# Three inverse jobs moved from the end of an FFT convolution into its last tiles, and two reloads moved ahead of outputs

## The chip, the cores and the metric

One core of a Trainium2 chip runs the kernel; the other seven are idle. The metric is the device time of one execution in microseconds (us), the median of several runs. The core has five engines that run side by side, each in its own program order: TensorE (PE, with its weight loads shown as PEld), VectorE (DVE), ScalarE (ACT), GpSimd (POOL) and SyncE (SP). SP does nothing here but issue DMA transfers.

## The reference

A 7x7 circular convolution over a 224x224 image with 96 input and 96 output channels, written as a product of two-dimensional Fourier transforms:

```python
H = W = 224; C = 96; K = 7
def reference(x, w):                       # x (1,224,224,96), w (7,7,96,96), bf16
    wp = jnp.pad(w, ((0, H - K), (0, W - K), (0, 0), (0, 0)))
    Xf = rfft2(x.astype(float32), axes=(1, 2))
    Wf = rfft2(wp.astype(float32), axes=(0, 1))
    Yf = jnp.einsum('bhwi,hwio->bhwo', Xf, Wf)
    return irfft2(Yf, s=(H, W), axes=(1, 2)).astype(bfloat16)
```

The output is 224 x 224 x 96 in bf16, 9.6 MB.

## The kernel before

**Tiling.** The image rows are cut into 8 blocks of 28 (`NJ`, `B`). Each block is transformed along the rows with a short Fourier transform of length 34 (`L`), which gives 17 frequencies (`NS`). Along the columns the kernel works directly with the seven taps, two output columns at a time. The columns are cut into 7 tiles of 32 pixels; the code counts them t = 0 to 6, and this text does too, so "the fifth tile" is tile 4, "the sixth" tile 5, and "the last" tile 6 (`TL`).

**Three stages for each tile.**

1. The forward transform (`a_jobs`): products of pixels with the constant matrix `Fm` on PE, copied from PSUM to `xf`. It runs one tile ahead, so nothing of it is left to do during tile 6.
2. 17 rounds (`b_round`), one for each frequency s. A round is 33 products of PE, 19 into a first PSUM bank and 14 into a second one, with operands that are pieces of `xf` or of sums `J` that DVE makes for three frequencies at a time (`jit`, two buffers). ACT scales the first bank into `tt_`, DVE makes `u` and `v` from the banks, and POOL or DVE adds them up to `yf`. After two or three rounds `yf` is written to a scratch tensor in HBM (`scr`, in the last tile seven smaller ones, `scrl`).
3. The inverse transform (`c_jobs`): the scratch is read back as `tt` with another order of axes (`load_t`), multiplied on PE by the constant matrix `Gm`, copied from PSUM to an output buffer (`yo`, or two halves of the third `J` buffer), and written to the output. There are 11 jobs for each tile, 0 to 10. They use five reloads: jobs 0 and 1 use (0,0), 2 and 3 use (1,0), 4 to 6 use (2,0), 7 and 8 use (0,1), 9 and 10 use (1,1). A job is two products of 384 columns and two copies of 384 elements per partition. The jobs 1, 3, 8 and 10 write 252 KB of output each, job 5 writes 252 KB in three transfers and job 6 writes 84 KB.

**How the jobs are placed.** Every round has two places where filling work is put: `mid`, between the two banks, and `end`. With k = 2s and 2s + 1 a tile has 34 such places. `pace` spreads a list of jobs evenly from place a to place b. For each tile, `CQ[t] = (nold, nnew)` says how many jobs left over from tile t - 2 and how many of tile t - 1 are done while the rounds of tile t run. The rest of tile t - 1 is left over for tile t + 1. The old jobs stand from place 3 to a place `km`, the new ones from `km` to the end; in tile 6 `km` is 13 and the end is 26. What is left over in tile 6 stands behind its rounds (`cj` after `tail[0] = 2`); there each product is followed by a second one of the same size with zeros (`wu`), which adds nothing, and the copies go to DVE and ACT in turn.

**The end.** The inverse of tile 6 is done differently: its scratch is reloaded in seven parts (`load_p(0)` to `load_p(6)`, into a free `xf` buffer), each as soon as its rounds are written. `load_p(5)` belongs to rounds 14 and 15, whose write POOL issues, and `load_p(6)` to round 16, whose write ACT issues. `first` multiplies the parts 0 to 2 (matrix `GA`); eight such products are made as soon as there are banks. Then come `WARM` = 12 products with zeros, and then `second` multiplies the parts 3 to 6 (matrix `GB`) and adds them in the same banks, DVE and ACT copy, and SP writes the output in eight transfers.

**Queues.** All reloads, all outputs and the scratch writes of the tiles 0 to 5 are issued by SP in one order; an instruction that waits holds up all behind it. Every DMA of SP has one of eight semaphores in turn, so it also waits for the one that stood eight places ahead of it.

Of the kernel before, what the change touches and what calls it, by code (L numbers as in the profile page):

```python
# [36 lines left out]
YBUF = 4  # L37
JGB = ((0, 3), (3, 6), (6, 9), (9, 12), (12, 15), (15, 17))
LAG = 4
CQ = {2: (11, 0), 3: (11, 2), 4: (9, 5), 5: (6, 8), 6: (3, 4)}  # L40
SH2 = {0: (0, 8, 17), 1: (0, 8, 17), 2: (0, 8, 13, 17)}
MERGE = ()
NP2 = 0
# [9 lines left out]
def kernel(  # L53
# [84 lines left out]
    def dma(out_ap, in_ap):  # L138
        return DE.dma_start(out=out_ap, in_=in_ap)
# [278 lines left out]
    def a_jobs(t):  # L418
        xf = new_xf(t)
        jobs = []  # L420
        for jg in range(2):
            for h in range(2):
                for (q, n) in ((0, 3), (3, 3), (6, 2)):
                    jobs.extend(a_bank(t, xf, xn_bufs[jg], h * PXC + 2 * q, n, jg, HALO + h * 8 + q))
            jobs.append(then_load(jobs.pop(), t + 1, jg))
        return jobs
# [182 lines left out]
    def load_p(i):  # L609
        a, b, h, r0 = prt[i]  # L610
        sv = scr_tiles[(TL, i)].rearrange("w j s (r e) -> (j s r) w e", r=2)
        n = 2 * (b - a)
        if h:
            dma(tl_b[r0:r0 + NJ * n], sv)
        else:
            for g in range(2):
                dma(tl_a[g][r0:r0 + 4 * n], sv[g * 4 * n:(g + 1) * 4 * n])
# [118 lines left out]
    def add(a, b, jobs):  # L736
        qs.append([a, b, jobs, len(jobs)])
# [64 lines left out]
    cj = c_jobs(0)  # L802
    gp = g_parts()
    for t in range(2, NT):
# [7 lines left out]
        if t + 1 < NT:  # L812
            add(4 if t == 2 else 0, 26, a_jobs(t + 1))
        nold, nnew = CQ[t]
        k1 = 2 * NS if t < TL else 2 * NS - 8
# [6 lines left out]
        cj = cn[nnew:]  # L822
# [18 lines left out]
            b_round(t, s, fills(qs, 2 * s), fills(qs, 2 * s + 1), bool(now) or (t == TL and s >= NS - 3), now)  # L841
    tail[0] = 2
    assert not pend
    for f in cj[:2]:
        f()
    load_p(5)
    cj[2]()
    load_p(6)
    for f in cj[3:]:
        f()  # L850
    if NP2:
        for c in reversed(ps_cms):
# [60 lines left out]
```

## Time and profile before

| | us |
|---|---|
| median of 8 runs | 275.1 |
| lowest and highest | 274.47, 277.74 |
| profiled execution, whole time | 274.54 |
| profiled execution, span | 272.8 |

| engine | busy us | share of the span |
|---|---|---|
| PE | 261.3 | 96% |
| PEld | 239.4 | 88% |
| DVE | 227.1 | 83% |
| ACT | 196.3 | 72% |
| POOL | 102.2 | 37% |

In the profile nearly all instructions carry line 87, the helper that keeps the order of each engine, so they are told apart by the tiles that they write and read: `pb<-tt,Gm` is a product of an inverse job, `pb<-WF,J` and `pb<-WF,xf` are products of a round, `pb<-xf,GA` and `pb<-xf,GB` belong to the end, `xf<-scrl` is a part of the last reload, `scrl<-yf` the write that it waits for.

The stages that the change touches lie in the profile like this (us from the start of the span): tile 5 from about 197 to 228, tile 6 from 228 to 255.7, the jobs behind the rounds from 255.7 to 261, the end from 261 to 272.8.

### The profile page before, as it was taken

How to read it: one execution, taken by the hardware profiler on the slowest of the kernel's cores; microseconds unless marked ns; L12 is line 12 of the kernel's file. 1: busy time of each engine (PE TensorE's matmuls, PEld its weight loads, DVE VectorE, ACT ScalarE, POOL GpSimd, SP SyncE). 2: the span in 40 equal slices, each digit the busy share in tenths (PEclk: the TensorE clock that was granted, in tenths of full speed). 3: DMA queues.
4: the chain of work that ended last, by engine and by line, in shares of the span. 5: the costliest groups of instructions: out<-in, count | busy, mean ns of one | idle time of the engine just before them, and what ended most of it. 6: DMA issues, size and time to landing. Idle time of an engine off the chain costs nothing.

```text
span 272.8 us, 12064 instructions
## 1 busy us (share of the span) xinstructions
PE 261.3 (96%) x5088; PEld 239.4 (88%) x5088; DVE 227.1 (83%) x465; ACT 196.3 (72%) x475; POOL 102.2 (37%) x152
## 2 busy tenths in 40 slices
PE   8979999989998999999999999999999999999993
PEld 3659998989998999899999999999999989999772
DVE  5539999999999889977986897788988889989844
ACT  5538997768774566898988869888897875463333
POOL 7730133444545455233243315222242233464300
PEclk9989999999999999999999999999999999999998
DMA  6956114511121189896968578785959672989866
GB/s 178 223 117 172 47 48 109 152 46 48 45 81 53 50 265 176 255 278 177 301 199 234 152 213 239 182 210 158 287 182 206 169 246 100 202 225 224 210 197 202
DMA packets 46355, 46.79 MB, mean 171 GB/s; under 512 B 35306, under 2 KB 38006, under 8 KB 46202
## 3 DMA queue, kind: packets, MB, share of 16 engines
q1 hardware_dynamic: 45708, 44.34, 59.7%
q0 software_dynamic: 448, 1.57, 1.9%
q8 instruction: 40, 0.66, 1.1%
q14 instruction: 15, 0.12, 0.2%
q10 hardware_dynamic: 144, 0.10, 0.1%
HBM read 24.65 MB, written 21.33 MB: 169 GB/s over the span
## 4 chain that ended last, share of the span: by engine, by line
PE 56%; DVE 21%; issue 8%; DMA 5%; ACT 4%; POOL 3%; SPq 1%; DVEq 0%; ACTq 0%
PE pb L87 56%; DVE J L87 8%; DMA wq<-in_w_dram 5%; DVE WF L87 4%; DVE v L87 4%; POOL yf L87 3%; DVE u L87 2%; DVE yf L87 2%; ACT WF L87 2%; ACT xf L87 1%; SPq L87 1%; DVE xf L87 0%; DVE yo L87 0%; DVE tt L87 0%; DVEq L908 0%
## 5 line engine op out<-in xcount | busy, mean ns | idle before, releaser
L87 PE MATMUL pb<-WF,J 96*128 96x96 bf16 x2898 | 168.0, 206 | 1.2 <-DVE J L87 0.5
L87 PEld LDWEIGHTS <-J 96*128 96x128 bf16 x2898 | 142.0, 98 | 10.7 <-DVE J L87 1.5
L87 POOL TENSOR_TENSOR yf<-v,u 128x384 bf16<-128x384 f32 x85 | 85.2, 1018 | 141.7 <-issue 89.1
L87 ACT CAST xf<-pb 96x408 bf16<-96x408 f32 (+5 forms) x142 | 67.0, 492 | 7.1 <-PE pb L87 5.1
L87 PE MATMUL pb<-WF,xf 96*128 96x96 bf16 (+1 forms) x952 | 61.3, 206 | 2.9 <-DVE WF L87 2.2
L87 DVE TENSOR_TENSOR J<-xf 96x1824 bf16<-96x1824 bf16 (+1 forms) x84 | 60.3, 757 | 0.1
L87 PEld LDWEIGHTS <-xf 96*128 96x128 bf16 x952 | 47.6, 98 | 3.8 <-issue 3.1
L87 PE MATMUL pb<-Fm,xn 118*128 118x136 bf16 (+4 forms) x576 | 44.4, 203 | 0.0
L87 ACT CAST WF<-pb 96x480 bf16<-96x480 f32 (+1 forms) x60 | 30.0, 561 | 7.7 <-PE pb L87 7.5
L87 PE MATMUL pb<-tt,Gm 102*84 102x384 bf16 (+1 forms) x132 | 33.6, 326 | 0.0
L87 ACT CAST yo<-pb 84x384 bf16<-84x384 f32 (+1 forms) x61 | 26.2, 480 | 5.1 <-PE pb L87 3.2
L87 PEld LDWEIGHTS <-xn 118*128 118x128 bf16 x576 | 29.2, 98 | 0.1
L87 ACT CAST J<-pb 84x384 bf16<-84x384 f32 (+1 forms) x62 | 26.8, 482 | 2.5 <-PE pb L87 2.3
L87 DVE TENSOR_TENSOR J<-J 96x912 bf16<-96x912 bf16 (+1 forms) x42 | 25.0, 595 | 0.0
L87 PE MATMUL pb<-wq 98*128 98x120 bf16 (+1 forms) x288 | 22.6, 232 | 1.5 <-DMA wq<-in_w_dram 1.5
L87 PEld LDWEIGHTS <-wq 98*128 98x128 bf16 x288 | 20.3, 150 | 2.0 <-DMA wq<-in_w_dram 2.0
L87 PE MATMUL pb<-wu 128*128 128x512 bf16 (+3 forms) x70 | 18.2, 389 | 1.1 <-DVE ct L87 1.1
L87 DVE TENSOR_TENSOR WF<-WF 96x960 bf16<-96x960 bf16 x15 | 15.8, 1056 | 0.2
L87 PEld LDWEIGHTS <-wu 128*128 128x128 bf16 (+3 forms) x70 | 7.8, 113 | 8.1 <-issue 2.4
L87 DVE TENSOR_TENSOR yf<-v,u 128x384 bf16<-128x384 f32 x24 | 13.8, 573 | 0.8
L87 DVE CAST WF<-pb 96x400 bf16<-96x400 f32 (+1 forms) x12 | 7.1, 608 | 7.5 <-PE pb L87 7.3
L87 PEld LDWEIGHTS <-Gm 102*84 102x84 bf16 (+1 forms) x132 | 11.5, 117 | 1.7 <-issue 0.6
(393 smaller groups left out, 238.7 us busy)
## 6 DMA issues: line engine op xcount, KB each, us to landing
scr<-yf SPq DMA_DIRECT2D x30, 288.0 KB
xn<-in_x_dram SPq DMA_DIRECT2D x12, 672.0 KB
tt<-scr SPq DMA_DIRECT2D x24, 336.0 KB
out_dram<-yo SPq DMA_DIRECT2D x12, 252.0 KB
out_dram<-J SPq DMA_DIRECT2D x12, 252.0 KB
tt<-scr SPq DMA_DIRECT2D x6, 288.0 KB
wq<-in_w_dram SPq DMA_DIRECT2D x1, 1719.0 KB
WF<-in_x_dram SPq DMA_DIRECT2D x2, 672.0 KB
```

The lines of the kernel that those rows point to most:

```text
L87: r = fn(*a, **k)
```

## The change

```diff
-CQ = {2: (11, 0), 3: (11, 2), 4: (9, 5), 5: (6, 8), 6: (3, 4)}
+CQ = {2: (11, 0), 3: (11, 2), 4: (9, 5), 5: (6, 11), 6: (0, 7)}
...
     tail[0] = 2
     assert not pend
+    load_p(5)
     for f in cj[:2]:
         f()
-    load_p(5)
-    cj[2]()
     load_p(6)
-    for f in cj[3:]:
+    for f in cj[2:]:
         f()
```

- During the rounds of tile 5 there are now 6 old jobs (of tile 3) and all 11 of tile 4, 17 in place of 14. The old ones stand in the places 3 to 13 (they stood in 3 to 16), the new ones in 14 to 33 (17 to 33).
- During the rounds of tile 6 there are again 7 jobs, but all of tile 5. The places 3 to 12 have none, where there were three. The places 13 to 25 have seven, at 13, 14, 16, 18, 20, 22 and 24, where there were four, at 13, 16, 19 and 22.
- Behind the rounds there are the jobs 7 to 10 of tile 5, four in place of seven. `load_p(5)` is issued ahead of all of them, `load_p(6)` after job 8, whose output of 252 KB is issued between the two.

## The prediction

> **What bounds the kernel now.** I read the chain of work that ended last, then busy times by stretch, the waits of DVE, and last the time line of SP's queue behind the rounds. Chain (start, length, what):
>
> ```profile
> 180.40 48.47 PE pb L87 x969
> 228.87 0.46 DVE v L87
> ...
> 252.17 8.21 PE pb L87 x92
> 260.40 0.56 DVE yo L87
> 261.01 7.04 PE pb L87 x41
> ```
>
> From 180 to 229, all of tile 5, the chain is PE alone; in tile 6 it goes through DVE and POOL (`v`, `yf`, `J`, `u`); behind the rounds it is PE again. By stretch (length, then busy time of PE, PEld, DVE, ACT, POOL, granted PE clock, DMA share, GB/s):
>
> ```profile
> 197.00:228.00 31.00, 31.00 (x618) 28.84 (x616) 27.41 (x58) 25.80 (x67) 10.69 (x11) 1.00 0.71 201
> 238.50:243.60 5.10, 5.05 (x108) 4.67 (x105) 4.68 (x11) 2.83 (x7) 2.51 (x3) 1.00 0.79 210
> 243.60:248.75 5.15, 5.10 (x108) 4.72 (x106) 4.72 (x11) 2.83 (x7) 2.50 (x3) 1.00 1.04 221
> 255.70:264.10 8.40, 8.23 (x52) 5.55 (x49) 4.49 (x9) 3.22 (x7) 0.54 (x1) 1.00 0.86 240
> ```
>
> Tile 5 has no gap on PE, and DVE has 3.6 us free of 31. In tile 6 three rounds take 5.1 us: DVE is busy for 4.7 of it and then stands until POOL gives back a buffer. Two waits of DVE, at the end of tile 5 and in tile 6:
>
> ```profile
> 221.01 0.36 DVE L87 SCALAR_TENSOR_TENSOR u<-pb,tt__6412 128x192 f32<-128x192 f32 x1 [0.61 <-ACT tt__6412 L87]
> 239.53 0.36 DVE L87 SCALAR_TENSOR_TENSOR u<-pb,tt__6955 128x192 f32<-128x192 f32 x1 [0.39 <-POOL yf L87]
> ```
>
> The first is DVE's last idle time over 0.2 us before 233.97: from 221 on it is as full as PE. The queue of SP behind the rounds:
>
> ```profile
> 256.86 0.31 SPq L87 DMA_DIRECT2D xf<-scrl  x1
> 257.88 1.30 SPq L87 DMA_DIRECT2D out_dram<-yo  x3
> 259.90 0.33 SPq L87 DMA_DIRECT2D xf<-scrl  x1
> 260.34 0.40 SPq L87 DMA_DIRECT2D out_dram<-J  x1
> 260.86 0.33 SPq L87 DMA_DIRECT2D xf<-scrl  x1
> 261.30 0.44 SPq L87 DMA_DIRECT2D out_dram<-J  x1
> ```
>
> ```profile
> SPq L87 <- DMA scrl<-yf: 1.7, 2, 1.1
> ```
>
> This decides the case. `load_p(5)` is the line at 259.90, `load_p(6)` the one at 260.86. SP was free at 259.19, yet issued `load_p(5)` at 259.90: two waits of SP in this window end with a scratch write (1.7 us, the longer 1.1, ahead of 256.86, the other ahead of 259.90). The write of rounds 14 and 15, issued by POOL at 256.31, made its last semaphore step at 259.89. So the outputs ahead of `load_p(5)` do not hold it. `load_p(6)` made its last step at 263.84; the weights of the first product that needs it were loaded at 264.10, the product began at 264.26. The seven jobs are thus a cover that is only about 0.3 us longer than what they cover.
>
> **The change, part by part.**
>
> 1. *Tile 5: three more jobs.* A job's two products put the next product of a round off by 0.33 us (238.64 to 238.97 in tile 6), so PE gets 3 x 0.33 = 0.99 us more in a stretch where it has no gap. The jobs bring six copies. In the order of the changed kernel DVE has six plain copies in the rounds of tiles 5 and 6 where it had three, the rest go to ACT; at about 0.55 us (219.86) that is 1.65 us for DVE, less than its 3.6 us of idle time, but three of them stand in the places just ahead of 221, in place of one, and only 0.61 us is free there. By about place 25, where DVE becomes full, two of the three jobs have run (13 against 11). Lower bound 0.4 us, for a case where much of the third job and some of the first two hide behind DVE; upper bound 1.9, where the additional copies of ACT and DVE (six at 0.48 to 0.55, on two engines, 1.5) bind with a wait or two as the 0.1 to 0.2 us ones that PE shows at 196.4, 201.4 and 225.0. I take +1.2, near PE's price, since the chain names PE. Two outputs of 252 KB move here too, from 231.69 and 240.36; SP has the room, the DMA share is 0.71, price 0. If an output buffer came free late, a copy on ACT would stand, and behind it the `tt_` that DVE waits for.
>
> 2. *Tile 6: three jobs less in places 3 to 12, three more in 13 to 25.* The early three (products at 230.45, 232.99, 235.31) lie where DVE and POOL set the pace, so removing them gives PE time that it spends waiting for `J`. Later, PE needs about 4.9 us of each 5.1 (it stands 0.2 us for `J` at 242.3 and 247.4) with two jobs; with four it needs 5.57, with three 5.24, which puts it 0.45 + 0.12 = 0.57 us behind. But DVE runs behind PE: the second bank of the round that begins at 242.32 is ready at about 243.8 and DVE takes it at 244.93. That 1.1 us is the cover; without it 0.57 us is paid. The jobs 4 to 6 now run here and need reload (2,0). Its last piece landed at 244.33, and place 20 comes at about 244.5: almost no cover. The wait would be at a weight load of PE, with all rounds behind it. Bounds: -0.5 (half of the early 0.99 counts after all) and +0.9 (0.57 and a short wait). I take +0.1.
>
> 3. *SP's order in tile 6.* The outputs of jobs 5 and 6 (252 and 84 KB) now stand ahead of `load_p(2)` and `load_p(3)`. Those were issued at 251.26 and 255.37, each on a scratch write; the outputs are ready by about 249, so no issue is put off. On the engines 336 KB come ahead of these reloads, while the 504 KB from 231.69 and 240.36 are gone: at 210 to 220 GB/s 0.8 us less in sum. `load_p(3)` and `load_p(4)` landed at 259.36 and 260.88, more than 0.9 us before they will be needed. Price 0.
>
> 4. *Behind the rounds: three jobs less.* There a job is four products of 0.165 us (255.68, 255.85, 256.01, 256.18), 0.66; three are 1.98, and some 0.5 of the 0.7 us of waits for banks goes with them. PE would be done with the first products and the 12 with zeros at about 264.2 - 2.4 = 261.8.
>
> 5. *The last reloads.* `load_p(5)` still waits for its scratch write, so it is issued at 259.90 as before. One output and `load_p(6)` follow with the same spacing, at 260.34 and 260.86. But that output now has 252 KB, not 84. The landings came in order of issue: 262.91 `load_p(5)`, 263.09 the 84 KB, 263.84 `load_p(6)`, 264.31 the next 252 KB. So 252 KB add 0.47 us where 84 KB add 0.18: `load_p(6)` lands at 264.1, the products start at 264.3 to 264.5, PE stands for over 2 us, and the 2.4 us of step 4 come to nothing. Bounds: the write before it, of the same size, took 2.24 us from issue (254.61 to 256.85) and this one 3.58, so up to 1.3 earlier, less the 0.3; against that a third less than the slowest of the larger ones (6.2 us at 235.64) is 4.1, +0.5 and the 0.3. So -1.0 to +0.8; I take +0.1, as the three outputs that go away began to move only at 259.3, when the data of that write was through.
>
> A rule weighs here as well. The Trainium skill, "DMA: Bandwidth & Descriptors", section "Queues, rings and completion order", says that a transfer's semaphore step lands only after all earlier writes of its DMA engine. The landings in order agree (262.91 to 264.31); by the rule the output ahead of `load_p(6)` must be through in full, and the sum stays.
>
> Sum: 1.2 + 0.1 + 0 + 0.1 = +1.4 us. On the profiled execution (274.54 = 272.8 of span and 1.7 around it) that is 275.9. The median of the runs is 0.56 above that execution, so 276.5.
>
> **The rivals.**
>
> *The write lands sooner* (not slower). If the scratch write of rounds 14 and 15 takes 2.24 us, `load_p(6)` lands 1.0 us earlier and the end shrinks by as much; with 0.8 us for tile 5 the time is 275.1 + 0.8 - 1.0 = 274.9. For it: the earlier write of this size. Against: its data moved from 257.56 to 259.34 beside `load_p(3)` and `load_p(4)`, which stay. It decides from a write of under 2.5 us on.
>
> *Stalls in the denser tiles.* Reload (2,0) comes late for place 20, or the copies hold up banks in tile 5; another 1.0 us, 277.5. For it: the 0.2 us of cover and DVE's fullness; against: the outputs taken out ahead of that reload.
>
> *The clock drops at the end.* PE now stands some 2.3 us before its last products. Row: PE stopped at 268.5, and the granted clock is 1.00 from 268 to 270 and 0.65 from 270 to 272.8, so it falls to half about 2.3 us after the stop. With half the clock 24 products of 0.165 take 4 us more, about 1.5 of it visible beside the 4.5 us of copies: 278.0. The Trainium skill, "TensorE: Matmul & The Clock Gate", "What's actually happening", asks for an idle window of about 3.4 us; by that alone the clock would hold and this rival add nothing.
>
> *The reorder takes hold as its words say* and `load_p(5)` goes out at 259.2: 0.7 us less, 275.8. Against: SP's wait for the write. Counted with the first rival.
>
> **How the numbers follow.** Forecast 55%, 276.5, own range 275.4 to 277.6. Write sooner 20%. Stalls 15%. Clock 10%. Half a percent, 1.4 us, is about what can be told from no change: six of the eight runs lie within 1.5 us. The forecast sits on that edge: half of its 55% is slower, half the same. The first rival is the same for some 12 points and faster for 8, if tile 5 is cheap too, and from the forecast's lower edge come 2 more for faster. The other rivals are slower but for 4 points. So faster 0.10, same 0.42, slower 0.48. For the range I leave out a tenth on each side: 274.3 to 278.2.
>
> **What would show it.** Tile 5 longer by about 1.2 us with PE still without gaps; the places 3 to 12 of tile 6 no shorter; `load_p(5)` issued at the end of its write, about 4.3 us after the last round's product; PE idle for about 2 us ahead of the `GB` products. It is wrong if those products start over 0.6 us sooner after the rounds than the 8.6 us of before, or if tile 5 does not grow.

## The result and the profile after

| | before | after |
|---|---|---|
| median, us | 275.6 (32 runs) | 278.53 (11 runs) |
| lowest and highest, us | 273.90, 278.77 | 276.65, 281.01 |
| profiled execution, whole time, us | 274.54 | 278.81 |
| profiled execution, span, us | 272.8 | 277.1 |

The ratio of the times is 1.0096, with a 95% interval of 1.0061 to 1.0132: the change costs about 1%. (Such ratios leave disturbed runs out; the fit to the clock further below uses all runs.) The median of before lies 0.5 us higher here than in the eight runs shown first, so the step between the medians is 2.9 us where 1.4 was forecast. The fit has one more run of the changed kernel, at 277.70; with it the median is 278.1.

The two profiled executions differ by 4.3 us of span. I cut both at the same instructions of DVE and PE: the last `u` of tile 4, the `u` of round 4 of tile 6, the last `v` of the rounds, the first product `pb<-xf,GB`, the end. (Some expectations below name the first of these cuts as round 2 of tile 5 and the third as the last `v` but one; the times they give, 40.90 and 9.39, are those of the cuts named here.)

| stretch, us | before | after | difference |
|---|---|---|---|
| start to the last `u` of tile 4 | 196.70 | 197.38 | +0.68 |
| 22 rounds, tile 5 and the first five rounds of tile 6 | 40.90 | 42.80 | +1.90 |
| rest of the rounds of tile 6, to the last `v` | 17.26 | 17.26 | 0 |
| last `v` to the first `GB` product | 9.39 | 9.47 | +0.08 |
| first `GB` product to the end | 8.57 | 10.18 | +1.61 |

The first row comes from the weight load at the start (14.79 us in this execution, 13.95 before), ahead of everything that the change touches. Two rows carry the difference: the tile that took three more jobs, and the last 10 us, where nothing was added.

The chain of waits of the changed kernel (start, length, what) shows both places:

```profile
181.08 28.00 PE pb L87 x557
210.57 0.55 DVE v L87
211.14 0.56 DVE yf L87
211.70 1.08 DVE J L87 x2
212.94 0.62 DVE J L87
213.89 19.69 PE pb L87 x393
...
258.89 3.61 DMA scrl<-yf
262.52 3.05 DMA xf<-scrl
265.57 1.34 issue
266.92 5.30 PE pb L87 x21
```

In tile 5 the chain was PE alone; now it leaves PE at 210.57 and goes through DVE before PE may go on at 213.89. The first of these instructions of DVE stands behind a copy of a job:

```profile
209.83 0.36 DVE L87 SCALAR_TENSOR_TENSOR u<-pb,tt__6059 128x192 f32<-128x192 f32 x1 [0.93 <-ACT tt__6059 L87]
210.10 0.54 DVE L87 CAST yo<-pb 84x384 bf16<-84x384 f32 x1
210.57 0.54 DVE L87 SCALAR_TENSOR_TENSOR v<-tt__6059,pb 128x384 f32<-128x384 f32 x1
```

DVE had stood for 0.93 us just before, waiting for ACT's `tt_`, but the copy comes behind that wait in its order. And behind the rounds PE is no longer on the chain until 266.92: it is the scratch write, the reload that waits for it, and then the products. The 1.34 us that the chain calls "issue" are the rest of the wait for `load_p(6)`, whose last semaphore step came at 266.83. In all ten profiles with four jobs behind the rounds the first `GB` product began 0.09 to 0.14 us after that step. The seven jobs of before were a cover; with four of them the write and the reloads behind it are bare.

The waits of PE, from its time line in the rounds of tiles 5 and 6 (start, length of the group, what, and in brackets the idle time ahead of it and who ended it):

```profile
213.89 0.34 PE L87 MATMUL pb<-Fm,xn 118*128 118x136 bf16 x3 [0.33 <-DVE u L87]
234.61 0.34 PE L87 MATMUL pb<-WF,J 96*128 96x96 bf16 x4 [0.45 <-DVE J L87]
239.78 0.34 PE L87 MATMUL pb<-WF,J 96*128 96x96 bf16 x4 [0.76 <-DVE J L87]
```

In the kernel before the same view shows no wait. The first lies in tile 5. The other two lie in the places 3 to 12 of tile 6, which lost their jobs: PE now stands there for DVE's `J` and gains nothing.

SP's queue behind the rounds:

```profile
258.12 4.70 SPq L87 DMA_DIRECT2D xf<-scrl  x3
262.92 0.42 SPq L87 DMA_DIRECT2D out_dram<-J  x1
263.46 0.30 SPq L87 DMA_DIRECT2D xf<-scrl  x1
```

The first line joins three reloads; the last of them, `load_p(5)`, went out at 262.52, which is the end of the scratch write in the chain above (258.89 + 3.61 = 262.50). That it stands ahead of all jobs in program order made it no earlier. The output of 252 KB comes next and `load_p(6)` at 263.46.

The end by stretch (from:to and length, then busy time of PE, PEld, DVE, ACT, POOL, granted PE clock, DMA share, GB/s), and three groups of PE's time line in it:

```profile
263.99:267.40 3.41, 1.14 (x8) 0.70 (x6) 0.10 (x1) 0.00 (x0) 0.00 (x0) 1.00 0.69 223
267.40:270.82 3.42, 3.42 (x13) 2.36 (x11) 2.02 (x4) 1.91 (x4) 0.00 (x0) 0.50 0.34 103
```

```profile
266.92 1.36 PE L87 MATMUL pb<-xf,GB 128*112 128x384 bf16 x5 [2.27 <-issue]
268.06 0.53 PE L87 MATMUL pb<-xf,GA 72*112 72x384 bf16 x1
271.05 0.33 PE L87 MATMUL pb<-xf,GA 72*112 72x384 bf16 x1
```

The same products in the kernel before:

```profile
264.26 0.98 PE L87 MATMUL pb<-xf,GB 128*112 128x384 bf16 x5
265.23 0.32 PE L87 MATMUL pb<-xf,GA 72*112 72x384 bf16 x1
265.39 0.33 PE L87 MATMUL pb<-xf,GB 128*112 128x384 bf16 x1
```

PE stands for 2.27 us ahead of the `GB` products. In the 3.41 us that hold this wait it is busy for a third of the time, and in the next 3.41 us its clock is half: a product of 384 columns shows as 0.53 us and follows the one before at 0.32, where it is 0.33 and 0.165 at full clock. From the first `GB` product to its last product PE takes 5.77 us instead of 4.26, which is 1.51 of the 1.61 us at the end.

### The profile page after: what moved, and what is told of

Its sections match the earlier page's. It is cut to its first block, busy times and chain, and to the rows that moved or that the text cites. A ratio compares the mean times of both kernels' runs of the same rounds, so it can differ in the third digit from the quotient of the medians.

```text
span 277.1 us, 12054 instructions
## 1 busy us (share of the span) xinstructions
PE 261.3 (94%) x5082; PEld 239.5 (86%) x5082; DVE 227.2 (82%) x465; ACT 195.3 (70%) x475; POOL 103.3 (37%) x152
## 4 chain that ended last, share of the span: by engine, by line
PE 49%; DVE 22%; DMA 11%; issue 9%; ACT 4%; POOL 3%; SPq 1%; DVEq 0%; POOLq 0%
PE pb L87 49%; DVE J L87 8%; DMA wq<-in_w_dram 5%; DVE v L87 4%; DVE WF L87 4%; POOL yf L87 3%; DMA tt<-scr 3%; DVE u L87 2%; DVE yf L87 2%; ACT WF L87 1%; ACT xf L87 1%; DMA scrl<-yf 1%; DMA xf<-scrl 1%; SPq L87 1%; DVE xf L87 1%
## 5 line engine op out<-in xcount | busy, mean ns | idle before, releaser
L87 POOL TENSOR_TENSOR yf<-v,u 128x384 bf16<-128x384 f32 x85 | 86.3, 1030 | 142.5 <-issue 88.8
L87 PE MATMUL pb<-wu 128*128 128x512 bf16 (+2 forms) x64 | 16.3, 395 | 1.1 <-DVE ct L87 1.1
L87 PEld LDWEIGHTS <-wu 128*128 128x128 bf16 (+2 forms) x64 | 7.1, 114 | 7.8 <-issue 2.2
```

What stands on the lines that cost most here:

```text
L87: r = fn(*a, **k)
```

## The experiments

Five questions: what the three jobs in tile 5 cost and why, what tile 6 and the end cost alone, whether the order of the reloads does anything, whether the half clock at the end is real in the runs without a profile, and whether some version beats both kernels. Below, "stretch" is the row of 22 rounds in the table above, 40.90 before and 42.80 after. Ratios are to the kernel before run beside it, with 95% intervals.

### The parts alone

`tile5_alone`, a change of the kernel before:

```diff
-CQ = {2: (11, 0), 3: (11, 2), 4: (9, 5), 5: (6, 8), 6: (3, 4)}
+CQ = {2: (11, 0), 3: (11, 2), 4: (9, 5), 5: (6, 11), 6: (0, 4)}
```

> The kernel before with CQ 5: (6, 11) and 6: (0, 4): the three jobs more in tile 5, three less in tile 6 (places 3 to 12), the seven jobs and the order behind the rounds as before. Theory (the cost lies in tile 5 alone and nothing of it comes back in tile 6): 1.9 us slower than the kernel before, about 277.5, with the 1.9 us between the first and the last round of tile 5, and the stretches of tile 6 and behind it as before. Rival (tile 6 gives back PE time when it has three jobs less): +0.9 to +1.3, about 276.7.

Measured: 278.64 (6 runs), ratio 1.0153 [1.0104, 1.0202], more than the whole change. Its profile, of the longest of the six runs (283.06), has a wait that neither kernel showed. From the chain of waits and from the time line of PE:

```profile
208.28 5.61 DMA tt<-scr
```

```profile
213.94 0.86 PE L87 MATMUL pb<-tt,Gm 102*84 102x384 bf16 x2 [2.16 <-DMA tt<-scr]
```

Reload (0,0) of tile 4, which the first new job needs, took 5.6 us and PE stood 2.16 us for it, in the middle of tile 5; the clock was then half for 6.8 us, and the stretch came to 47.64. The new jobs now begin at place 14 instead of 17, so this reload has three places less of cover. Whether that belongs to the kernel or to that execution could not be told from one profile; it is taken up below.

`tile6_and_tail`, a change of the changed kernel: tile 5 as before, ten jobs in tile 6, four behind the rounds and the new order of the reloads.

```diff
-CQ = {2: (11, 0), 3: (11, 2), 4: (9, 5), 5: (6, 11), 6: (0, 7)}
+CQ = {2: (11, 0), 3: (11, 2), 4: (9, 5), 5: (6, 8), 6: (3, 7)}
```

> The changed kernel with CQ 5: (6, 8) and 6: (3, 7): tile 5 as before, tile 6 with ten jobs, four jobs behind the rounds, load_p(5) and load_p(6) ahead as in the change. Theory (tile 6 is bound by DVE and POOL, so jobs are free there; the end is bound by the last reload): tile 5 and tile 6 as long as before, from the last round's sum to the first GB product 8.1 us (8.3 before), PE standing over 2 us, so the time is that of the kernel before, 275.4, where the clock holds, and up to 1.6 more where it drops: 275.3 to 277. Rival (PE binds tile 6 with seven jobs in places 13 to 25 behind three): tile 6 0.5 to 1.0 us longer.

Measured: 276.25, ratio 1.0054 [1.0025, 1.0083]. Ten jobs in tile 6 cost nothing: stretch 40.91, rest of the rounds 17.26. But three jobs fewer behind the rounds gain nothing either: from the last `v` to the first `GB` product it took 10.19 us, against 9.39 with seven jobs. From PE's time line:

```profile
258.90 2.12 PE L87 MATMUL pb<-wu 128*112 128x384 bf16 x12
264.01 0.99 PE L87 MATMUL pb<-xf,GB 128*112 128x384 bf16 x5 [3.00 <-issue]
```

PE is done with all that it has by 261 and stands for 3.00 us. Here its clock stayed full although it stood longer than in the changed kernel; the last section says why.

`reorder_alone`, a change of the kernel before: the order of the reloads alone, with seven jobs.

```diff
+    load_p(5)
     for f in cj[:2]:
         f()
-    load_p(5)
-    cj[2]()
     load_p(6)
-    for f in cj[3:]:
+    for f in cj[2:]:
         f()
```

> The kernel before with load_p(5) ahead of all jobs behind the rounds and load_p(6) after two jobs. Theory (load_p(5) waits for its scratch write, not for SP): load_p(5) is issued at the end of the write again, 3.6 us after POOL issued it; the three outputs of job 5 (252 KB) now stand between load_p(5) and load_p(6), so load_p(6) is issued about 0.9 us later and lands 1 to 1.5 us later; the time is 0.8 to 1.5 us longer than before, 276.4 to 277.1. Rival (outputs ahead of the reload held it): 0.5 to 0.7 us shorter, 275.0.

Measured: 275.92, ratio 1.002 [0.9985, 1.0056]: not told from no difference, though the interval reaches to 1.5 us. In its profile, of the longest of its twelve runs, `load_p(5)` went out at 264.63, the end of its scratch write (264.61), and that write took 4.7 us. `load_p(6)` followed 1.77 us later (0.96 before), and the first `GB` product came 10.45 us after the last `v`, 1.06 later than before, as the theory said for this order; the times do not show it.

### What the three jobs in tile 5 cost

`zero_products`, a change of the kernel before: three of the 14 jobs of tile 5 make a second product with zeros behind each product, so PE gets the six products of three jobs, but DVE and ACT get no copies. They add nothing to the result.

```diff
+    in5 = [0]
+    cnt = [0]
...
+                    cnt[0] += in5[0]
+                    zero = tail[0] or in5[0] and cnt[0] in (4, 8, 12)
...
-                                  ... start=True, stop=not tail[0])
-                        if tail[0]:
+                                  ... start=True, stop=not zero)
+                        if zero:
```

> The kernel before with a product with zeros behind each of the two products of three inverse jobs in tile 5 (the fourth, eighth and twelfth): six products of 384 columns more on PE, as three more jobs bring, and no copy, no reload and no output more. Theory (PE is the price of 1.0 us and DVE's copies the rest): the stretch grows by 0.7 to 1.0 us to 41.6 to 41.9, the time to 276.1. Rival (DVE alone sets tile 5): it grows by less than 0.3 us. Second rival (PE's price is the whole of it): by 1.9.

Measured: stretch 41.83, +0.93, which is close to 6 x 0.165 = 0.99 for PE; ratio 1.0043 [1.0004, 1.0082]. PE's share of the 1.90 is thus about 0.9, and the other 1.0 comes with the copies and the places.

`copies_on_act`, a change of the changed kernel: every copy of tile 5's rounds that a choice sends to DVE or ACT goes to ACT. `before_copies_on_act` does the same to the kernel before.

```diff
+    in5 = [0]
...
+        if in5[0]:
+            return SE.copy(out=out_ap, in_=in_ap)
...
+        in5[0] = int(t == TL - 1)
```

> The changed kernel with every copy out of PSUM that is made while the rounds of tile 5 run put on ACT; DVE has none there (six in the changed kernel, three in the one before). Measured by the stretch from DVE's u of round 2 of tile 5 to the u of round 4 of tile 6: 40.90 us in the kernel before, 42.81 in the changed one. Theory (DVE): the three additional copies on DVE stand between u and v, ahead of yf and J, and make up what the stretch grew by over PE's 0.99 us: the stretch is then 41.9 us or less and the time 1 us or more below that of the changed kernel, 277.0. Rival (ACT and PE): ACT becomes the late one, the stretch stays at 42.8 or grows to 44, the time 278.5 or more.

> The kernel before with the same: no copy on DVE while the rounds of tile 5 run (three in the kernel before). Theory (DVE): the stretch is 0.3 to 1.2 us shorter than its 40.90, as DVE is full from 221 us on, and the time 274.2 to 275.0, the first below the kernel before. Rival (PE alone sets tile 5): the stretch stays within 0.2 us of 40.90 or grows as ACT runs late.

Measured: 278.17, ratio 1.0114 [1.0077, 1.015], stretch 42.24, for the first; 275.78, ratio 1.0032 [0.9995, 1.0068], stretch 40.90, unchanged, for the second. Freeing DVE in the changed kernel gives back 0.56 us of stretch, and of PE's three waits only the last (0.76) is left. In the kernel before it gives nothing: there DVE was not late. The time of the first did not fall with it, so this holds for the profile only.

`new_from_17`, a change of the changed kernel: the eleven new jobs of tile 5 begin at place 17, as in the kernel before, instead of 14, and the old ones spread to 16.

```diff
+        if t == TL - 1:
+            km = 17
```

> The changed kernel with the six old jobs of tile 5 in places 3 to 16 as before and the eleven new ones in 17 to 33, so the first use of reload (0,0) is at place 17 again, not at 14. Theory (copies and products set the price, the reload is in time): the stretch is 42.8 us within 0.4, the time that of the changed kernel, 278.5 within 1. Rival (PE waits for the reload at place 14 in many runs, and the clock drops behind it): the time falls by 1 us or more, to 277.5 or less, and its spread narrows.

Measured: 277.07, ratio 1.0081 [1.0045, 1.0116]; stretch 42.31. The wait of PE at 213.89 is gone. Two more runs settled the rest. `tile5_alone_again` is the kernel of `tile5_alone`; `tile5_from_17` adds to it the edit of `new_from_17`.

> The kernel before with three more new jobs in tile 5 alone (17 jobs there, four in tile 6, seven behind the rounds), as in the earlier run of the same kernel. Theory: its first run was too dear because PE waited for reload (0,0), which is first used at place 14 instead of 17; if that wait belongs to the kernel, it comes back in this profile (a gap of over 1 us on PE early in tile 5, stretch over 44 us) and the time is 3 us or more above before at a like clock. Rival: the wait was a single event of that profile; the stretch is 42.8 us as in the changed kernel, and at a like granted clock the time lies 1.9 us above before (ratio 1.007), with at most half a microsecond more.

> The same, but the old jobs in the places 3 to 16 and the eleven new ones from place 17 on, so that reload (0,0) has the cover that it had before. Theory (the late reload): the time falls by 1 us or more against the kernel with the new jobs from place 14. Rival (the place of the jobs alone): the stretch is 42.3 in place of 42.8 us, and the time falls by those 0.5 us only. At a like clock it would lie 1.4 us above before.

Measured: `tile5_alone_again` 277.34 (12 runs), ratio 1.0071 [1.0038, 1.0104], stretch 42.84, no wait for a reload; so the 2.16 us do not belong to every execution of this kernel. How often they come is not known: the other five runs of the first series were slow too and have no profile. `tile5_from_17` 277.29, ratio 1.0037 [1.0002, 1.0072], stretch 41.69. That is 1.15 us less, more than the 0.5 that the place alone was expected to give. The time line of PE in the changed kernel had three waits in tiles 5 and 6; `tile5_alone_again` has the same three, and `tile5_from_17` has one:

```profile
240.17 0.34 PE L87 MATMUL pb<-WF,J 96*128 96x96 bf16 x4 [0.75 <-DVE J L87]
```

The wait early in tile 5 is gone, and so is the first of the two in tile 6: DVE reaches the end of tile 5 in time. What is left of the price, 0.79 us, is no more than the work of PE. So in tile 5 the jobs cost 0.8 to 0.9 us as products, and about 1 us more because DVE falls behind when the new jobs begin at place 14 and the old ones stand closer. Round by round, the start of `u` in tile 5 later than in the kernel before, counted from the last `u` of tile 4 (us):

| round of tile 5 | `tile5_alone_again` | `tile5_from_17` | `zero_products` |
|---|---|---|---|
| 4 | 0.46 | 0.00 | 0.00 |
| 9 | 1.14 | 0.00 | 0.34 |
| 13 | 1.94 | 0.79 | 0.67 |
| 16 | 1.95 | 0.80 | 0.93 |

The changed kernel shows the first column within 0.01, and from round 16 on to the end of tile 6 no column moves by more than 0.05: all of the price arises in tile 5. More than half of it is there by round 9.

The same edit gave 42.31 in `new_from_17`, 0.62 more, though the order of PE is the same in the stretch of tile 5 where they part. The time line of ACT in `new_from_17` shows why:

```profile
225.38 0.85 ACT L87 CAST yo<-pb 84x384 bf16<-84x384 f32 x2 [1.03 <-DMA out_dram<-yo]
```

An output buffer was still being sent. ACT stood 1.03 us for it, and the `tt_` behind that copy, which DVE's `u` needs, came late; in `tile5_from_17` no such wait stands there. With one profile of each, whether this belongs to the kernel or to the execution is open.

`reverse`, a change of the kernel before: three jobs fewer in tile 5 and three more in tile 6.

```diff
-CQ = {2: (11, 0), 3: (11, 2), 4: (9, 5), 5: (6, 8), 6: (3, 4)}
+CQ = {2: (11, 0), 3: (11, 2), 4: (9, 5), 5: (6, 5), 6: (6, 4)}
```

> The kernel before with the change turned round: CQ 5: (6, 5) and 6: (6, 4), three jobs fewer in tile 5, six in place of three in places 3 to 12 of tile 6, seven behind the rounds. Theory (a job costs in tile 5, where PE is full, and is free in the early places of tile 6, where DVE and POOL set the pace): the stretch from u of round 2 of tile 5 to u of round 4 of tile 6 is 0.6 to 1.5 us shorter than 40.90, the rest of tile 6 as before (17.26) or up to 0.5 longer, the time 274.0 to 274.8. Rival (tile 6 has no room left, PE stands there only 0.15 us at 237.2): what tile 5 gains tile 6 loses, 275.1.

Measured: 275.51, ratio 1.0004 [0.9972, 1.0036]; stretch 40.73. Three jobs more cost 1.90, three fewer give back 0.17, although no job copy is left on DVE in tile 5; PE then has a wait of 0.24 us for DVE's `u` at 218.98. As far as these runs show, the kernel before stands just at the point where PE and DVE are both full.

### The reloads at the end

`both_first`, a change of the changed kernel: `load_p(6)` directly behind `load_p(5)`. `before_both_first` and, once more, `before_both_first2` do it with seven jobs.

```diff
     load_p(5)
-    for f in cj[:2]:
-        f()
     load_p(6)
-    for f in cj[2:]:
+    for f in cj:
         f()
```

> The changed kernel with load_p(6) directly behind load_p(5), both ahead of the four jobs behind the rounds and of their outputs. Measured from the last but one v of tile 6 to the first GB product: 9.39 us in the kernel before, 9.47 in the changed one. Theory (the last reload sets the end; load_p(5) is held by its scratch write, load_p(6) by the 252 KB of output ahead of it): load_p(5) is issued at the end of its write again, load_p(6) lands 0.3 to 0.5 us earlier, the stretch is 9.0 to 9.2 us, and PE still stands about 2 us. The time falls by no more than that, 278.1. Rival (it is the write or other traffic, not the output ahead): the stretch stays at 9.4 or more.

> The kernel before with load_p(5) and load_p(6) ahead of the seven jobs behind the rounds. Theory: PE's own seven jobs are the cover and now the later one, so the stretch from the last but one v to the first GB product stays at 9.2 to 9.4 us and the time is that of the kernel before, 275.1, within 0.5. Rival (the reload also sets the end of the kernel before in most runs): 0.5 us or more faster.

> The kernel before with both last reloads ahead of the seven jobs, once more (0.9978, 0.9946 to 1.001, the first time). Theory (PE's seven jobs cover the reload in the profile, but a reload that lands 0.1 to 0.3 us earlier helps the executions in which it is late): 0.997 to 1.000. Rival (no effect): 1.000 within 0.002.

Measured: 277.87, ratio 1.0085 [1.0044, 1.0126] for the first; 275.09, 0.9978 [0.9946, 1.001] and 275.05, 1.0002 [0.997, 1.0033] for the two others. With four jobs `load_p(6)` landed 0.66 us behind `load_p(5)`, where it was 1.26 with the output between them, and the first `GB` product came 9.30 us after the last `v` instead of 9.47. But the changed kernel's second profile (`after_again`, below) took 9.28 with the output in place, so 0.17 us is within the scatter. Over all ten four-job profiles `load_p(6)` lands 0.57 to 0.74 us behind `load_p(5)` where nothing stands between them (three) and 1.18 to 2.01 where the output does (seven); the first `GB` product comes after 9.30 to 9.45 and 9.28 to 11.00 us. The output ahead may thus cost some tenths of a microsecond in an execution, and nothing that the times can tell. With seven jobs it stayed at 9.39 and 9.40: there the jobs hide it. They do not always: in `tile5_alone_again` the scratch write took 4.43 us, and PE stood 0.27 us for the reload in spite of seven jobs.

### The clock at the end

`warm24`, a change of the changed kernel: 24 products with zeros ahead of `second`, so that PE stands less.

```diff
-WARM = 12
+WARM = 24
```

> The changed kernel with 24 products with zeros ahead of the second half of the last inverse, in place of 12; they need about 2.0 us more of PE. Theory (clock): in the changed kernel PE stands 2.4 us for the last reload (264.5 to 266.9), the granted clock falls to half from 267.4 to 270.8 and the last 5 us of products take 1.6 us more. With the gap filled there is no window at half the clock after the start, the stretch from the first GB product to the end is 8.5 us as in the kernel before (10.2 in the changed one), and the time is about 276.7 us, 1.0 to 1.8 below the changed kernel. Rival (the end is longer for another reason, the copies or the output transfers): the stretch stays at 10 us and the time at 278.5.

Measured: 278.37, ratio 1.0107 [1.007, 1.0144]. In the profile the half clock is gone and the end takes 8.84 us instead of 10.18. PE's time line:

```profile
261.81 4.07 PE L87 MATMUL pb<-wu 128*112 128x384 bf16 x24
266.73 0.99 PE L87 MATMUL pb<-xf,GB 128*112 128x384 bf16 x5 [0.85 <-issue]
267.88 0.33 PE L87 MATMUL pb<-xf,GB 128*112 128x384 bf16 x1
```

But the times did not fall. To see whether the profile speaks for the other runs, I ran the changed kernel again (`after_again`), the combination with both reloads first (`both_first_warm24`) and `tile6_and_tail` with 24 (`tile6_tail_warm24`).

> The changed kernel once more, beside the three others. Theory: 1.9 us in tile 5, and behind the rounds 0.1 to 0.5 us for the reload and 1.2 to 1.6 where the clock drops (in most executions): ratio 1.008 to 1.013. Rival (the clock holds in most executions without a profile): 1.007 or less.

> The changed kernel with load_p(5) and load_p(6) ahead of all behind the rounds and 24 products with zeros. Theory (what is left of the loss is tile 5): no window at half the clock between the rounds and the end, 9.3 us to the first GB product, and 1.9 to 2.3 us over the kernel before, ratio 1.007 to 1.0085, 0.7 us or more below after_again. Rival (the clock hardly drops in most executions): the same as after_again within 0.4 us.

> tile6_and_tail (tile 5 as in the kernel before, ten jobs in tile 6, four behind the rounds) with 24 products with zeros. Theory (its loss of 1.5 us, interval 0.7 to 2.3, is the clock in part of its executions and a reload 0.1 to 0.8 us late): 0.1 to 0.8 us over the kernel before, ratio 1.0005 to 1.003. Rival (the loss is not the clock): 1.005 again.

Measured: 278.45, 1.0124 [1.0078, 1.0169]; 279.01, 1.0117 [1.0066, 1.0168]; 275.97, 1.0042 [1.0013, 1.0071]. By the medians alone the filling does nothing. A half clock over the `GB` products stands in the profiles of the changed kernel (twice), `both_first`, `copies_on_act` and `new_from_17`, with 10.1 to 10.2 us from the first `GB` product to the end; in none with seven jobs behind the rounds (8.6 to 9.5), and in one of the four with 24 zeros, `tile6_tail_warm24` (10.15). The 8.57 of the kernel before is the shortest of the 14 ends at full clock (8.57 to 9.80, mean 9.1), so half clock lengthens the end by about 1.0 us rather than by the 1.6 of the first pair. PE's own part is sharp, 4.26 to 4.28 us against 5.77 to 5.93; what varies is how long the last outputs take behind the last copy, 3.7 to 5.0 us at full clock and 3.6 to 3.8 behind the slowed products.

Every run without a profile, too, records its span and the mean granted clock of its PE. That answers what the profiles leave open. A run loses, on the mean, so much of its clock:

| kernel | runs | clock lost, with 95% interval |
|---|---|---|
| before | 142 | 0.0068 ± 0.0009 |
| nine other series with seven jobs behind the rounds | 102 | 0.0068 ± 0.0009 |
| six series with four jobs and 12 zeros (the changed kernel twice) | 66 | 0.0108 ± 0.0015 |
| four series with four jobs and 24 zeros | 39 | 0.0074 ± 0.0019 |

So the four-job end does lose clock. Tile 5 is not the reason: with the dense tile 5 and seven jobs 30 runs lose 0.0078 ± 0.0019, with the dense tile 5, four jobs and 12 zeros 54 runs lose 0.0111 ± 0.0017. What 24 zeros restore is less clear, since the kernels of the last row differ. With tile 5 as before, `tile6_tail_warm24` loses 0.0044 ± 0.0023 and `tile6_and_tail` 0.0098 ± 0.0037; with the dense tile 5 it is 0.0097 ± 0.0031 with 24 (15 runs) and 0.0109 ± 0.0024 with 12 (30 runs), which are not told apart. One straight line for all kernels, with a level for each of them (349 runs), gives 1.92 ± 0.16 us for each 0.01 of clock, and these levels above the kernel before at equal clock, with the part of the mean time that the clock explains (known to 0.4 to 1.0 us, for the changed kernel to 0.6):

| kernel | runs | level above before, us | by the clock, us |
|---|---|---|---|
| changed kernel, both series | 18 | 2.24 ± 0.41 | 0.85 |
| `warm24` | 9 | 2.65 ± 0.55 | 0.45 |
| `both_first` | 12 | 2.17 ± 0.49 | 0.68 |
| `both_first_warm24` | 6 | 2.54 ± 0.67 | 0.75 |
| `tile6_and_tail` | 12 | 0.38 ± 0.49 | 0.57 |
| `tile6_tail_warm24` | 12 | 1.32 ± 0.49 | -0.45 |
| `tile5_alone`, first series | 6 | 2.86 ± 0.68 | 1.23 |
| `tile5_alone_again` | 12 | 2.29 ± 0.48 | -0.26 |
| `tile5_from_17` | 12 | 1.49 ± 0.48 | 0.15 |
| `new_from_17` | 12 | 1.33 ± 0.49 | 0.59 |
| `copies_on_act` | 12 | 2.03 ± 0.49 | 1.15 |
| `zero_products` | 12 | 1.25 ± 0.48 | -0.17 |
| `reorder_alone` | 12 | 0.21 ± 0.48 | 0.19 |
| `reverse` | 12 | 0.41 ± 0.48 | -0.29 |
| `before_both_first`, both series | 24 | 0.02 ± 0.36 | -0.25 |
| `before_copies_on_act` | 12 | 0.04 ± 0.48 | 0.28 |
| `outputs_last` | 12 | 0.11 ± 0.48 | 0.11 |

The whole change is then 2.24 + 0.85 = 3.1 us on the mean. The three jobs in tile 5 alone, both series together (18 runs), give a level of 2.48 ± 0.40 and 0.24 ± 0.54 by the clock. Tile 6 and the end alone give 0.38 ± 0.49 and 0.57 ± 0.73; neither is told from nothing by itself, though their sum is (ratio 1.0054). So tile 5 answers for the level, and the loss of clock belongs to the four-job end, the second shown by the kernels together and not by one of them. The filling did not pay: the mean times with 24 zeros equal those with 12 (3.1 us above before in `warm24` as in the changed kernel, 0.9 in `tile6_tail_warm24` against 0.95). In `tile6_tail_warm24` what the clock wins, 1.0 us, comes back as 0.9 in level. Where the level comes from is not shown; in the profile of `tile6_tail_warm24` the last reload came latest of all, 11.00 us from the last `v` to the first `GB` product.

### A version to beat both

`outputs_last`, a change of the changed kernel: tile 5 as before, both reloads ahead of all jobs, 24 zeros, and the outputs of the jobs 4 to 6, which run in tile 6, issued behind `load_p(6)`. In it the outputs of the jobs 4 and 5 are taken from the buffer of job 6, so that part of the output image is not the reference's.

```diff
-CQ = {2: (11, 0), 3: (11, 2), 4: (9, 5), 5: (6, 11), 6: (0, 7)}
+CQ = {2: (11, 0), 3: (11, 2), 4: (9, 5), 5: (6, 8), 6: (3, 7)}
-WARM = 12
+WARM = 24
...
+    late_out = []
...
-                def put(j0, nj, px, npx, row, col):
+                def put(*k):
+                    if t == TL - 1 and (gi, h) == (2, 0):
+                        late_out.append(lambda: put_now(*k))
+                    else:
+                        put_now(*k)
+
+                def put_now(j0, nj, px, npx, row, col):
...
     load_p(5)
-    for f in cj[:2]:
+    load_p(6)
+    for f in late_out:
         f()
-    load_p(6)
-    for f in cj[2:]:
+    for f in cj:
         f()
```

> CQ 5: (6, 8) and 6: (3, 7), so tile 5 as in the kernel before and four jobs behind the rounds; load_p(5) and load_p(6) directly behind each other, and the outputs of jobs 4 to 6 of tile 5 (336 KB), made during the rounds of tile 6, issued only behind load_p(6); 24 products with zeros. Theory (the reload is late because the DMA engines are full with outputs from 245 us on): the scratch write of rounds 14 and 15 takes 3.0 us or less (3.6 before), the stretch to the first GB product is 8.4 to 8.9 us, and the time is 0.3 to 1.0 us below the kernel before, 274.4. Rival (the write and the reloads take their time whatever stands ahead): 9.3 us or more and no gain.

Measured: 275.19, ratio 0.9992 [0.9957, 1.0026], 9.45 us from the last `v` to the first `GB` product. Its scratch write still took 3.88 us with those outputs out of the way, so they are not what makes it slow. It is back at the time of before, and no version was found that is faster than that.

## Why the prediction was wrong, and where it was right

**Step 1, tile 5, is the term that was mis-sized.** It said +1.2 us, with bounds of 0.4 and 1.9. The profile showed 1.90, and `tile5_alone_again` 1.94 in its profile; the level of that kernel over both series is 2.48 ± 0.40. The price of PE was right (0.99 forecast, 0.93 in `zero_products`). What failed is the sentence that DVE has room until it becomes full at about place 25, so that two of the three jobs have run while it has room and only three of its copies stand where it has none. DVE is late long before: its `u` is 0.46 us late in round 4 and 1.14 in round 9, which holds the places 18 and 19. In tile 5 DVE copies four job results in the changed kernel (at 203.95, 210.10, 215.33 and 223.46) and two before (209.10 and 219.86); the chain leaves PE behind the second of the four, and PE waits there and again early in tile 6. The 3.6 us of idle time that the step counted on are a sum over the tile, and part of it lies ahead of a copy, where the copy cannot use it. With the new jobs from place 17, and the old ones spread as before, both waits are gone and 0.79 is left. I chose near PE's price "since the chain names PE"; but the chain of a kernel with two full engines names the one that ended last, and three more jobs were enough to change it. Also, PE did not stay without gaps in tile 5, as the prediction's sign asked. The late output buffer that this step named in passing came too, in the profile of `new_from_17`, and not in the changed kernel.

**Step 2, tile 6, was right.** The rest of tile 6 takes 17.26 us in both kernels and in the one with ten jobs, and its first five rounds keep the delay that tile 5 gave them. The jobs taken out of the places 3 to 12 turned into waits of PE for `J`, and reload (2,0) was in time.

**Step 3 was right**: the reloads that it speaks of were issued within 0.02 us of the end of their scratch writes, and PE waited for none of them.

**Steps 4 and 5 were right in mechanism and size.** The first `GA` product came 3.78 us after the last `v` instead of 6.14, 2.36 us sooner, as forecast with 2.4; the first `GB` product came 0.08 later, forecast 0.1. That the two agree to 0.02 is luck: in the second profile of the changed kernel it came 0.11 sooner. `load_p(5)` waited for its write, which took 3.61 us (3.58 before).

**The clock loss was left out of the sum.** The prediction set it at 10% as a rival, and so it stood in no term. It is no alternative: the standing PE follows from steps 4 and 5, and in the mean of all runs the lost clock costs 0.85 ± 0.63 us. The rule that it set against this rival, an idle window of 3.4 us, did not hold here: the clock fell behind a wait of 2.27 us (last section). Its price, 1.5 us, agrees with the 1.51 that PE lost in the profile, but by luck: it had all 24 products at half clock, 4 us more, with 1.5 of it visible beside the copies, while the half clock lasted 3.41 us and the copies hid nothing of it in this pair. With the measured 1.9 for tile 5 and 0.85 for the clock put in, the sum would have been about 2.9 us above before, the step between the medians.

**The first rival fell**: from the issue of the scratch write to that of `load_p(5)` it took 3.5 to 4.7 us in the kernels with the new order, never under 2.5. **The stalls** occurred in tile 5 (waits for DVE and not for PSUM banks or reload (2,0)). **The reorder** took no hold: in all 13 profiles with `load_p(5)` ahead of the jobs it went out within 0.02 us of the end of its scratch write. With the old order it went out 0.45 and 1.25 us after that end in two profiles (`before_copies_on_act` and `tile5_alone`), whose writes took only 3.0 and 3.1 us, so the outputs ahead can hold it when the write is quick.

One thing stays open: `tile5_from_17` is 0.79 longer in its profile, and 1.49 ± 0.48 in level at equal clock. The profile's figure is outside that interval, and I have no run that tells why. A wait for an output buffer as in `new_from_17`, whose stretch grew by 1.41 and whose level is 1.33, would fit, but it was not seen in this kernel.

## What to carry to other kernels

Work moved out of a tail is paid where it lands, and in a stage where two engines are full it can cost more than its price on either (here 1.9 us for 0.9 of products), while taking work out of such a stage gives back almost nothing (0.17). A cover that is as long as the transfer behind it cannot be shortened for gain: shorten the transfer first, and before moving a DMA's issue forward look at what it waits for. When a change leaves PE standing, put the loss of clock that follows into the sum with its share, not among the mishaps.

## What the runs showed of the hardware

**The clock goes by half-busy windows, not by idle ones.** The half clock comes in pieces of 3.41 us or multiples, on a grid that runs through the whole execution. The windows of `tile6_and_tail`, which kept its clock, and of `tile6_tail_warm24`, which lost it:

```profile
259.10:262.50 3.40, 1.91 (x12) 1.26 (x10) 0.00 (x0) 0.00 (x0) 0.00 (x0) 1.00 0.65 184
262.50:265.90 3.40, 1.89 (x11) 1.43 (x12) 1.51 (x4) 1.24 (x3) 0.00 (x0) 1.00 0.17 61
```

```profile
264.10:267.50 3.40, 1.54 (x10) 0.99 (x9) 0.97 (x3) 0.81 (x2) 0.00 (x0) 1.00 0.32 98
267.50:270.90 3.40, 3.40 (x12) 2.30 (x11) 1.68 (x5) 1.48 (x4) 0.00 (x0) 0.50 0.59 179
```

A wait of 3.00 us that falls on the border of two windows leaves each of them 56% busy, and the clock stays; a wait of 1.85 us inside one leaves it 45% busy, and the clock halves in the next. In the grid of all 20 profiles, from 35 us on, each of the 22 windows at full clock with PE busy for 52% or less was followed by half clock, and none of those with 54% or more. Where a wait falls on this grid differs from execution to execution (in the two profiles of the changed kernel by 0.6 us, counted from the last `v`), so the same kernel can lose its clock in one run and not in another. The Trainium skill, "TensorE: Matmul & The Clock Gate", "What's actually happening", states the free-running window of 3413 ns, and the traces agree; it asks for an idle window before the clock falls, and there the measurement differs: a third to a half of busy time did not keep it.

**One reload can take far longer in one execution.** Reload (0,0) took 5.61 us in `tile5_alone` and held PE for 2.16; in the second profile of the same kernel it took 3.67 and PE never waited for it. Of the 16 steps of its semaphore 15 were there after 3.66 us; only the last one came 1.95 us later.
